# A fused attention and MLP kernel: weight sums of the last two groups taken straight from the joined weights, and the work of batch 0 placed anew

## Chip, cores and metric

The kernel runs on one core of a Trainium2 chip. The metric is device time in microseconds (us), the median of several executions. A core has five engines that work side by side and wait for each other through semaphores: TensorE (PE) for matmuls, VectorE (DVE) and ScalarE (ACT) for elementwise work, GpSimd (POOL) for elementwise work too, and SyncE (SP), which here only issues transfers. ACT issues some transfers as well. Each engine works through its own instructions in the order in which the program gives them.

## Reference

Clustered attention is followed by a mixing MLP. Queries and keys are each given to one of 16 clusters, and a query sees the keys of its own cluster only; the second part mixes tokens with a low rank matrix and then applies a two-layer MLP to each token. Shapes: 4 batches, 8 heads, 768 tokens, head dimension 64, model dimension 512, hidden dimension 2048.

```
scores = where(q_assign == k_assign, q @ k.T / 8, -1e9)
x = softmax(scores) @ v              # 4 x 768 x 512, heads side by side
u = x + ((x.T @ U) @ V).T            # U: 768 x 32, V: 32 x 768
out = u + relu(u @ w_ch1) @ w_ch2    # 512 x 2048 and 2048 x 512
```

U, V and both weight matrices are given as doubles.

## The kernel before

**Attention.** 16 units (batch times pair of heads), 12 steps each, make x batch by batch. Step numbers are the clock of the whole plan: M0 = 193 is the step at which batch 0's MLP begins, while the mixing of the last batch's tokens is still to come.

**The order.** A plan is written by hand: `at(time, function, arguments)` notes a call, all calls are sorted by their time and made in that order, and `keep_order` fixes that every engine keeps it. The times are numbers in tables (`mixes`, `stages`) and in the loops behind them. When something really runs follows from the waits: a function that stands early in an engine's order and has to wait holds up all that stands behind it on that engine.

**Precision.** A product in full precision is made of three matmuls: each operand is split into a high half, rounded to the matmul's format, and a low half, the rest (high x high, high x low, low x high). A matmul instruction is 128 x 128 against 384 or 512 columns.

**Batch 0's MLP.** It runs in two halves of 384 tokens (i = 0 and 1), each of 16 steps f, one for each 128 hidden units. A step has `gemm1(i, f)` (12 matmuls of 384 columns, L598 to L600), a relu on ACT that writes the high half of the hidden units (L606), the low half on DVE (L607), and `gemm2(i, f)` (9 matmuls of 512 columns, L617 to L619) that adds to y. In the plan gemm1 of the next step stands ahead of gemm2 of this one.

**The weights.** They come in four groups of four hidden blocks, and each group has eight tiles of 128 x 512, four of w1 and four of w2. `load_weights(g, step, stage)` makes a tile in four stages: a transfer of the doubles as 64-bit words (`rw`, L151, on ACT's queue for groups 2 and 3), a multiplication of the upper words on ACT (`rw_g`, L159), the `join` of both words on DVE (L169, L170, L172), whose result stands in PSUM (`ps_t`) for groups 2 and 3, and at last the high half as a cast on ACT and the low half as a subtraction on DVE (L190, L191). Groups 2 and 3, 16 tiles, are made in the first half of batch 0, one tile a step.

**The weight sums.** Batches 1 to 3 use a form with seven products in place of eight (Strassen's, in Winograd's variant), which needs sums and differences of quarters of the weights. A "turn" n makes them for one group g and one matrix k (0 for w1, 1 for w2). `recover` (L656 to L660) puts the weight together again from its halves, one quarter at a time: a copy of the low half to PSUM on ACT (L659), and an addition on DVE (L660) that writes a piece of the buffer `f`. `combine` (L662 to L671) makes four sums on POOL, `split_high` (L676) and `split_low` (L680) split them on ACT and POOL, and `store_sum` (L684, L685) writes both halves to the scratch `wc` in DRAM. Two of the places for high halves are the buffers `rw_t`. `store_block` (L643) writes the quarters that need no sum. The eight turns ran in the order of the groups, 3.1 steps apart from M0 + 3, the last one at M0 + 26.3.

**The tokens of batch 1.** `fetch_half` (L738) reads half of the mixed tokens into `st`, `turn_half` (L743) turns them on PE and copies them on ACT (L744), `u_sums` (L756) makes differences of quarters on DVE, in buffers of a ring to which `rw_t` belongs too, and `u_halves` (L761 to L767) splits quarters and differences on ACT and POOL. `fetch_w1` (L771) and `fetch_w2` (L783) read weight sums back. The low halves of batch 1's hidden units are made on POOL (L862).

**The last mix.** `mix_u`, `mix_sum` and `mix_v` for batch 3 run in the first half too: L533 to L550, with six additions on DVE into xt (L550) and a store to `u_scr`.

Of the kernel before, what the change touches and what calls it, by code (L numbers as in the profile page):

```python
# [40 lines left out]
B, H, S, D, C = 4, 8, 768, 64, 16  # L41
# [7 lines left out]
HT = NT // 2  # L49
ND = DM // P  # L50
NF = DF // P
NG = 4
# [35 lines left out]

mixes = {
    "mix_u":    ( 18.88,  18.35,  18.48,  16.57),  # L90
    "mix_sum":  ( 19.11,   19.1,  19.15,  18.35),
    "mix_v":    (  20.5,   20.4,  20.68,  19.42),
}


# [1 line left out]
    "mix":  (  3.36,   6.22,  15.04,  16.96),  # L97
    "g0":   ( 35.66,  38.22,  42.54,  52.94),
    "g1":   (-26.11, -21.73,  -20.5, -18.29),
    "g2":   ( -1.25,      0,    0.4,    0.7),  # L100
    "g3":   (  6.75,      8,    8.4,    8.7),
}

spots = [0.66, -0.06, 1.8, 2.25, 1.26, 2.09, 2.97, 3, 3.49, 3.81, 4.58, 5.03]
# [13 lines left out]
def clustered_attention_moe(ctx: ExitStack, tc: tile.TileContext, qk, v, cen, moe_U, moe_V, w1, w2, out):  # L118
# [3 lines left out]
    nc = tc.nc  # L122
# [21 lines left out]
    u_scr = [dram.tile([P, NT, DM], F32, name=f"u_scr{b}") for b in range(B)]  # L144

    def fetch(srcs, n, queue=nc.sync):

        step = srcs[0].shape[0]
        rw = raw.tile([P, 512], I64, name="rw")[0:step * len(srcs), 0:n]
        for i, src in enumerate(srcs):  # L150
            queue.dma_start(out=rw[i * step:(i + 1) * step], in_=src)  # L151
        return rw

    def upper(rw):

        r, n = rw.shape
        g = raw.tile([P, 512], F32, name="rw_g")[0:r, 0:n]
        high = rw.bitcast(I32).rearrange("p (n two) -> p n two", two=2)[:, :, 1].bitcast(F32)
        nc.scalar.mul(g, high, 2.0 ** -112)  # L159
        return rw, g.bitcast(I32)  # L160
# [15 lines left out]
    parts, pool = {}, {}  # L176

    def load_weights(g, step, stage):

        k, i = divmod(step, 4)  # L180
        if stage == 0:
            parts[g, step] = fetch([(w1, w2)[k][g, :, i, :]], 512, nc.scalar if g > 1 else nc.sync)
        elif stage == 1:
            parts[g, step] = upper(parts[g, step])
        elif stage == 2:
            parts[g, step] = join(*parts[g, step], g > 1)
        else:
            w = parts.pop((g, step))[2].bitcast(F32)
            hi, lo = wg[g][2 * k][:, i, :], wg[g][2 * k + 1][:, i, :]
            nc.scalar.copy(hi, w)  # L190
            (nc.vector if g > 1 or g == 1 and step in (1, 2, 3, 5) else nc.gpsimd).tensor_sub(lo, w, hi)  # L191


    def weight_tile(g, name, pool):
# [116 lines left out]
    n = B * NP  # L311
# [318 lines left out]
    B11, B12, B21, B22, T1, T2, T3, T4 = "B11", "B12", "B21", "B22", "T1", "T2", "T3", "T4"  # L630
# [10 lines left out]
    def store_block(k, g, name, part):  # L641

        nc.sync.dma_start(out=wc[k][g][:, :, slot[k][name], part * 256:part * 256 + 256],  # L643
                          in_=blocks(k, g, part)[name].bitcast(F32))

    def temps(n):
        at = 3072 * (n % 2 == 0 or n > 5)
        return [pool["f"][:, at + 512 * j:at + 512 * j + 512].rearrange("p (a n) -> p a n", a=2) for j in range(4)]

    def high_of(n, j):  # L650
        f = pool["f"]
        places = [f[:, 5120:5632], f[:, 5632:6144], *pool["o"], f[:, 2048:2560], f[:, 2560:3072]]
        count["o"] += 1
        return places[count["o"] % (6 if n < 6 else 4)].rearrange("p (a n) -> p a n", a=2)

    def recover(n, k, g, j):  # L656
        hi, lo = (blocks(k, g, part)[("A21", "A11", "A22", "A12")[j]] for part in range(2))
# [33 lines left out]
    spare, count = [], {"bank": 0, "f": 0, "o": 0}  # L691
# [43 lines left out]
        return ps[:, 0:HS]  # L735

    def fetch_half(b, h):
        nc.sync.dma_start(out=pool["st"], in_=u_scr[b][:, h * HT:(h + 1) * HT, :])  # L738

    def turn_half(b, h, d):  # L740
        ps = work("ps_uT")[:, 0:HS] if b == 1 else bank()
# [4 lines left out]
    def u_block(b, key):  # L746
        k, t = int(key[1]) - 1, int(key[2]) - 1
        return pool["ys"][1 - b % 2][:, 2 * k:2 * k + 2, t]
# [9 lines left out]
    def u_halves(b, key):  # L758
        if key[0] == "B":
            hi, lo = uc[key][:, 0], uc[key][:, 1]  # L760
            nc.scalar.copy(hi, u_block(b, key))  # L761
            nc.gpsimd.tensor_sub(lo, u_block(b, key), hi)
        else:
            for k in range(2):
                x = live["t", key, k]
                nc.scalar.copy(uc[key][:, 0, k], x)
                nc.gpsimd.tensor_sub(uc[key][:, 1, k], x, uc[key][:, 0, k])  # L767
# [168 lines left out]
    M0 = NS * n + 1  # L936
    plan = []

    def at(time, fn, *args):
        plan.append((time, len(plan), fn, args))  # L940
# [27 lines left out]
    for i in range(n):  # L968
# [10 lines left out]
        pace = (0.5, 0.75, 0.75, 1)[min(i, 3)]  # L979
        for u in range(NT if i == 0 else 0, NS):  # L980
            for h in range(2):
                if i < 3:
                    at(when("rowmax", i) + pace * u + 0.01 * h, rowmax, i, u, h)
                else:
                    g, r = divmod(2 * u + h, 2 * GV)
# [7 lines left out]
        for k in range(NS):  # L993
            h, c = divmod(k, NT)
# [10 lines left out]
    for b, (t_u, t_sum, t_v) in enumerate(zip(*mixes.values())):  # L1005
        o = NS * (NP * b + NP - 1)
        at(o + t_u, mix_u, b)
        at(o + t_sum, mix_sum, b)
        for t in range(NT):
            at(o + t_v + (t if b < B - 1 else t // HT), mix_v, b, t)  # L1010


    for k in range(3):
# [2 lines left out]
    for g, pace in enumerate((NS, 2.04, 1, 1)):  # L1016
        for stage, step in enumerate(stages[f"g{g}"]):
            for k in range(8):
                at(step + pace * k + (M0 if g else 0), load_weights, g, k, stage)

    at(M0 - 0.75, open_mlp)
    at(M0 + 8.05, open_weights)
# [8 lines left out]
            at(m + f + (1.2 if i == 0 or f < NF - 1 else 1.45), gemm2, i, f)  # L1031
        at(m + (16.35 if i == 0 else 16.47), finish, i)

    for n_, (g, k) in enumerate((g, k) for g in range(NG) for k in range(2)):
        c = M0 + (3 + 3.1 * n_ if n_ < 7 else 26.3)
        for r in range(4):
            at(c + 0.4 * r, recover, n_, k, g, r)
            at(c + (0.9, 1.4, 1.75, 2.1)[r], combine, n_, r)
            at(c + (1.9, 2.25, 2.6, 2.8)[r], split_high, n_, r)
            at(c + (2.4, 2.7, 3.0, 3.3)[r], split_low, n_, r)  # L1040
            at(c + (2.8, 3.1, 3.4, 3.7)[r], store_sum, n_, k, g, r)
        for r, name in enumerate(("A11", "A12", "A22")):
            for half in range(2):
                x = 2 * r + half
                since = (95, 142, M0 - 9, M0 - 2.5)
                at(since[n_] + (6 if g == 0 else 0.9) * x if g < 2 else M0 + 15.5 + 3.3 * (n_ - 4) + 0.55 * x,
                   store_block, k, g, name, half)

    at(M0 + 18, open_sevens)
    at(M0 + 31.3, free_rows)  # L1050
# [2 lines left out]
    for b in range(1, B):  # L1053
        o = M0 + NF * nh + 28 * (b - 1)
        if b == 1:
            fetched, turns = (o - 13.9, o - 6.4), (o - 7.7, o - 5.4)
        else:
            fetched, turns = (o - 20, o - 14), (o - 15.7, o - 8.7)
        for h in range(2):
            at(fetched[h], fetch_half, b, h)  # L1060
            for d in range(ND):
                at(turns[h] + 0.4 * d, turn_half, b, h, d)
        for k, key in enumerate((T1, T2, T3, T4)):
            for r in range(2):
                at((o - 4.9 if b > 1 else o - 3.9) + (k + 0.5 * r) * (1 if b > 1 else 0.8), u_sums, b, key, r)
        for key, when_ in ((B11, -4.95), (T1, -4.2), (B21, -3.7), (T2, -3.2), (B22, -2.7), (T3, -2.2), (T4, -1.2)):
            at(o + when_ * (1 if b > 1 else 0.8), u_halves, b, key)

        seq = [(1, 0), (1, 1), (1, 2), (2, 0), (1, 3), (2, 1), (1, 4), (2, 2), (1, 5), (2, 3),
               (1, 6), (2, 4), (1, 7), (2, 5), (2, 6), (2, 7)]  # L1070
        for k, (which, x) in enumerate(seq):
            t = o + 7 * U * k
            for s in range(7):
                if which == 1:
                    at(t + U * s, seven1, b, x, s)
                    at(t + U * s + 0.28, after1, b, x, s)
                else:
                    m, e = x // 2, 7 * (x % 2) + s
                    at(t + U * s, seven2, b, m, e)
                    at(t + U * s + 0.27, after2, b, m, e)  # L1080
            if which == 1:
                for key, sums, high, low in ((B22, None, 1.2, 1.25), (B11, None, 1.45, 1.5), (B21, None, 1.7, 2.6),
                                             (T3, 1.81, 2.0, 2.1), (T1, 1.95, 2.15, 2.4), (T2, 2.09, 2.3, 2.35),
                                             (T4, 2.23, 2.56, 2.6)):
                    if sums:
                        at(t + sums, h_sums, b, x, key)
                    at(t + high, h_high, b, x, key)
                    at(t + low, h_low, b, x, key)
                if x + 2 < 8 or b < B - 1:
                    for s0, s1 in ((0, 4), (4, 7)):  # L1090
                        at(t + U * s1 + 0.02, fetch_w1, (x + 2) % 8, s0, s1)
            elif x < 6 or b < B - 1:
                first = sorted(order[1].index(key) for key in order[b < B - 1][0:3])
                slots = [k for k in range(7) if (k in first) == (x % 2 == 0)]
                for K in range(2):
                    at(t + 7 * U + 0.01 * K, fetch_w2, (x - x % 2 + 2 + K) % 8, *slots)
        if b < B - 1:
            for j, when_ in enumerate((0.02, 0.1, 5, 5.3, 5.1, 5.45, 5.6, 5.9)):
                at(o + 28 + when_, join_up, b, j)
# [38 lines left out]
```

## Time and profile before

| | us |
|---|---|
| three executions | 1010.62, 1011.31, 1015.38 |
| their median | 1011.31 |
| the profiled execution | 1008.9 |
| its span in the profile | 1007.1 |
| batch 0's first half, first gemm1 to last gemm2 | 466.54 to 558.42 |
| batch 0's second half, up to batch 1's first product | 560.53 to 634.84 |

All rows are of the profiled execution, and their times count from the start of its span. A row of a timeline has its start, its duration, the engine, the line, and what it writes and reads; in brackets stands how long the engine was idle before it, and what ended that. A window gives the busy time of each engine in a stretch, and the TensorE clock that was granted as a share of full speed. In the list of waits, "y L617 <- ACT hx L606" reads: the matmul at L617 that writes y waited for ACT's row at L606 that writes hx. Matmuls overlap, so that their durations (0.34 and 0.40 us) are longer than their distances (0.174 and 0.232 us).

### The profile page before, as it was taken

How to read it: one execution, taken by the hardware profiler on the slowest of the kernel's cores; microseconds unless marked ns; L12 is line 12 of the kernel's file. 1: busy time of each engine (PE TensorE's matmuls, PEld its weight loads, DVE VectorE, ACT ScalarE, POOL GpSimd, SP SyncE). 2: the span in 40 equal slices, each digit the busy share in tenths (PEclk: the TensorE clock that was granted, in tenths of full speed). 3: DMA queues.
4: the chain of work that ended last, by engine and by line, in shares of the span. 5: the costliest groups of instructions: out<-in, count | busy, mean ns of one | idle time of the engine just before them, and what ended most of it. 6: DMA issues, size and time to landing. Idle time of an engine off the chain costs nothing. (4 is left out here: it accounts for less than half of the span.)

```text
span 1007.1 us, 15377 instructions
## 1 busy us (share of the span) xinstructions
PE 953.1 (95%) x5368; PEld 778.0 (77%) x5368; DVE 715.1 (71%) x1322; ACT 472.0 (47%) x837; POOL 601.5 (60%) x453
## 2 busy tenths in 40 slices
PE   5899999999999999988988998999999899999997
PEld 3565665676666756656777887899999899999997
DVE  5797777777787667666788524765688666886767
ACT  4454555565555645464456534453344433443330
POOL 5466676889678868753356846742375623855330
PEclk9899999999999999989999999999999999999999
DMA  7754653655676644347477995877677776677744
GB/s 183 193 130 119 162 148 93 201 156 151 152 213 170 153 116 144 96 134 235 142 232 232 322 349 187 329 266 271 231 261 260 274 295 239 229 280 267 248 147 146
DMA packets 76733, 205.29 MB, mean 204 GB/s; under 512 B 8624, under 2 KB 42416, under 8 KB 71792
## 3 DMA queue, kind: packets, MB, share of 16 engines
q1 hardware_dynamic: 73968, 195.82, 60.9%
q10 hardware_dynamic: 2688, 8.49, 2.8%
q8 instruction: 42, 0.69, 0.3%
q14 instruction: 35, 0.29, 0.1%
HBM read 131.07 MB, written 41.94 MB: 172 GB/s over the span
## 5 line engine op out<-in xcount | busy, mean ns | idle before, releaser
L442 DVE TENSOR_REDUCE m<-ps_max 128x1 f32<-128x384 f32 x384 | 195.5, 549 | 82.6 <-PE ps_max L440 81.2
L479 POOL TENSOR_TENSOR T<-T,pr 128x768 f32<-128x768 f32 x120 | 225.7, 1881 | 46.1 <-ACT pr L469 19.5
L469 ACT ACTIVATE pr<-st 128x768 f32<-128x768 f32 x192 | 154.6, 813 | 85.7 <-PE st L466 69.0
L487 PE MATMUL o_ps<-pr,vt 128*64 128x384 f32 x768 | 132.9, 496 | 0.1
L440 PE MATMUL ps_max<-arena 128*128 128x384 f32 x384 | 126.6, 380 | 6.7 <-DVE oh L356 2.5
L464 PE MATMUL st<-arena 128*128 128x384 f32 x384 | 105.0, 354 | 1.9 <-ACT pr L469 1.8
L440 PEld LDWEIGHTS ps_max<-arena 128*128 128x128 f32 x384 | 70.5, 192 | 45.4 <-issue 21.4
L487 PEld LDWEIGHTS o_ps<-pr,vt 128*64 128x64 f32 x768 | 52.9, 138 | 66.9 <-issue 60.3
L466 PE MATMUL st<-arena 97*128 97x384 f32 x384 | 99.7, 341 | 4.6 <-DMA arena<-mT 2.6
L479 POOL TENSOR_TENSOR T<-pr 128x768 f32<-128x768 f32 x30 | 56.6, 1885 | 64.9 <-ACT pr L469 64.9
L464 PEld LDWEIGHTS st<-arena 128*128 128x128 f32 x384 | 66.3, 190 | 17.8 <-issue 9.9
L466 PEld LDWEIGHTS st<-arena 97*128 97x128 f32 x384 | 70.4, 190 | 6.2 <-issue 4.5
L491 ACT COPY os<-o_ps 128x384 f32<-128x384 f32 x32 | 15.4, 480 | 105.4 <-PE o_ps L487 105.4
L800 PE MATMUL ps_p<-arena,w 128*128 128x384 f32 x186 | 62.3, 335 | 0.1
L801 PE MATMUL ps_p<-arena,w 128*128 128x384 f32 x186 | 62.2, 334 | 0.0
L802 PE MATMUL ps_p<-arena,w 128*128 128x384 f32 x186 | 62.2, 334 | 0.0
L800 PE MATMUL ps_q<-arena,w 128*128 128x384 f32 x150 | 50.1, 334 | 0.0
L802 PE MATMUL ps_q<-arena,w 128*128 128x384 f32 x150 | 50.1, 334 | 0.0
L801 PE MATMUL ps_q<-arena,w 128*128 128x384 f32 x150 | 50.1, 334 | 0.0
L380 POOL TENSOR_TENSOR arena<-R,arena 128x768 fp32r<-128x768 f32 x18 | 34.4, 1918 | 13.5 <-ACT arena L375 7.9
L665 POOL TENSOR_TENSOR f<-f 128x512 f32<-128x512 f32 x8 | 10.3, 1293 | 52.1 <-DVE f L660 52.1
L607 DVE SCALAR_TENSOR_TENSOR hx<-ps_h,hx 128x384 fp32r<-128x384 f32 x32 | 17.7, 554 | 29.0 <-ACT hx L606 28.9
(541 smaller groups left out, 2444.3 us busy)
## 6 DMA issues: line engine op xcount, KB each, us to landing
w<-wc SPq DMA_DIRECT2D x24, 1024.0 KB
w<-wc SPq DMA_DIRECT2D x24, 768.0 KB
wc<-f SPq DMA_DIRECT2D x52, 256.0 KB
arena<-wc SPq DMA_DIRECT2D x17, 768.0 KB
R<-in_qk SPq DMA_DIRECT2D x32, 384.0 KB
arena<-arena SPq DMA_DIRECT2D x32, 384.0 KB
arena<-arena SPq DMA_DIRECT2D x64, 192.0 KB
arena<-wc SPq DMA_DIRECT2D x10, 1024.0 KB
```

The lines of the kernel that those rows point to most:

```text
L380: eng.tensor_sub(part(X2[i % 3], 0, h), live["R", i][:, 2 * h:2 * h + 2].rearrange("p j q -> p (j q)"), part(X1[i % 3], 0, h))
L440: nc.tensor.matmul(ps[:, 0:HS], x1[:, 0, g // 2, g % 2, t * P:(t + 1) * P], x1[:, 1, h, g % 2, :], start=True, stop=True)
L442: nc.vector.reduce_max(live["m2", i][:, h, u:u + 1], ps[:, 0:HS], axis=AX.X)
L464: nc.tensor.matmul(st[:, j, 0:HS], x1[:, 1, hk, j, ks], x1[:, 0, h, j, :], start=True, stop=False)
L466: nc.tensor.matmul(st[:, j, 0:HS], x2[0:97, 1, hk, j, ks], x2[0:97, 0, h, j, :], start=False, stop=True)
L469: nc.scalar.activation(pr, st[:, :, 0:HS], AF.Exp, scale=SCALE)
L479: eng.tensor_add(T, live["p", i, h, 0] if c == 1 else T, live["p", i, h, c])
L487: nc.tensor.matmul(o_ps[64 * j:64 * j + 64, 0:HS], vv[:, c, j, :], pr[:, j, :], start=(c == 0), stop=(c == NT - 1))
L607: nc.vector.scalar_tensor_tensor(out=hl, in0=ps[:, 0:HS], scalar=0.0, in1=hh, op0=ALU.max, op1=ALU.subtract)
L800: nc.tensor.matmul(ps, w[:, 0, k], u[:, 0, k], start=(k == 0), stop=False)
L801: nc.tensor.matmul(ps, w[:, 0, k], u[:, 1, k], start=False, stop=False)
L802: nc.tensor.matmul(ps, w[:, 1, k], u[:, 0, k], start=False, stop=(k == 1))
```

## The change

**Sums from the joined weights.** `keep_joined` is new. For groups 2 and 3 it copies the joined weight on ACT straight from PSUM to the places in `f` from which `combine` starts. `recover` remains for groups 0 and 1 alone; 16 copies and 16 additions of it go, and 16 copies come. The turns of groups 2 and 3 come first (`turns_of`); as their tiles must be joined first, turn 0 stands at M0 + 2.5, and each next one four steps later. Groups 0 and 1 follow in the second half. `temps` and `high_of` are changed to fit the new places.

**The joins** of groups 2 and 3 start earlier in their steps (`stages`), and the first two loads three steps earlier still.

**The last mix** has its second part 0.7 steps earlier, and its six last products two by two, from 18.42 on, where they stood three by three from 19.42.

**The tokens of batch 1.** The fetch of half 1 is issued by ACT in place of SP, and the turning of both halves is placed anew. The subtraction for one quarter (B11) goes from POOL to DVE.

**The last turn.** Its `combine`, `split` and `store` parts wait 5.9 steps more, and so stand behind the start of batch 1's products. `store_block` has new times.

```diff
 mixes = {
-    "mix_sum":  ( 19.11,   19.1,  19.15,  18.35),
-    "mix_v":    (  20.5,   20.4,  20.68,  19.42),
+    "mix_sum":  ( 19.11,   19.1,  19.15,  17.65),
+    "mix_v":    (  20.5,   20.4,  20.68,  18.42),
...
-    "g2":   ( -1.25,      0,    0.4,    0.7),
-    "g3":   (  6.75,      8,    8.4,    8.7),
+    "g2":   ( -1.75,  -0.44,  -0.28,   0.25),
+    "g3":   (  6.25,   7.56,   7.72,   8.25),
...
             nc.scalar.copy(hi, w)
             (nc.vector if g > 1 or g == 1 and step in (1, 2, 3, 5) else nc.gpsimd).tensor_sub(lo, w, hi)
+            if g > 1:
+                keep_joined(turns_of.index((g, k)), i, w)
...
+    turns_of = [(2, 0), (2, 1), (3, 0), (3, 1), (0, 0), (0, 1), (1, 0), (1, 1)]
+
+    def keep_joined(n, i, w):
+
+        at = 3072 * (n % 2 == 0)
+        f = pool["f"][:, at:at + 2048].rearrange("p (c k a n) -> p c k a n", c=2, k=2, a=2)
+        to = f[:, i // 2, :, i % 2] if n % 2 else f[:, :, 1 - i // 2, i % 2]
+        nc.scalar.copy(to, w.rearrange("p (c n) -> p c n", c=2))
...
-        nc.sync.dma_start(out=pool["st"], in_=u_scr[b][:, h * HT:(h + 1) * HT, :])
+        (nc.scalar if b == 1 and h else nc.sync).dma_start(out=pool["st"], in_=u_scr[b][:, h * HT:(h + 1) * HT, :])
...
-            nc.gpsimd.tensor_sub(lo, u_block(b, key), hi)
+            (nc.vector if b == 1 and key == B11 else nc.gpsimd).tensor_sub(lo, u_block(b, key), hi)
...
-            at(o + t_v + (t if b < B - 1 else t // HT), mix_v, b, t)
+            at(o + t_v + (t if b < B - 1 else 0.45 * t), mix_v, b, t)
...
-                at(step + pace * k + (M0 if g else 0), load_weights, g, k, stage)
+                ahead = 3 if g == 2 and stage == 0 and k < 2 else 0
+                at(step + pace * k + (M0 if g else 0) - ahead, load_weights, g, k, stage)
...
-    for n_, (g, k) in enumerate((g, k) for g in range(NG) for k in range(2)):
-        c = M0 + (3 + 3.1 * n_ if n_ < 7 else 26.3)
+    for n_, (g, k) in enumerate(turns_of):
+        c = M0 + (2.5, 6.5, 10.5, 14.5, 17.3, 20.0, 22.7, 26.4)[n_]
+        if n_ > 3:
+            for r in range(4):
+                at(c + 0.3 * r, recover, n_, k, g, r)
+        wait = 5.9 if n_ == 7 else 0
         for r in range(4):
-            at(c + 0.4 * r, recover, n_, k, g, r)
-            at(c + (0.9, 1.4, 1.75, 2.1)[r], combine, n_, r)
...
+            at(c + wait + (0.9, 1.4, 1.75, 2.1)[r], combine, n_, r)
...
-            fetched, turns = (o - 13.9, o - 6.4), (o - 7.7, o - 5.4)
+            fetched, turns = (o - 13.9, o - 6.45), (o - 7.9, o - 5.1)
```

**What moves, in three places.** The rows that follow give line, operation, what is written and read, and the shape; a DMA row is the issue of a transfer. Line numbers are each kernel's own.

First place: ACT, in the first steps of the first half. `hx` are relus, `rw` loads of a later tile, `rw_g` the multiplied upper words, `arena<-ps_t` the high cast. Before:

```order
L159 ACTIVATE rw_g<-rw 128x512
L501 COPY sums<-ps_sum 128x384
L606 ACTIVATE hx_5005<-ps_h 128x384
L190 CAST arena<-ps_t 128x512
L151 DMA rw<-in_w 128x512
L159 ACTIVATE rw_g<-rw 128x512
L606 ACTIVATE hx_5006<-ps_h 128x384
```

and of the change, for the second tile, with the kept copy at L655:

```order
L608 ACTIVATE hx_5007<-ps_h 128x384
L159 ACTIVATE rw_g<-rw 128x512
L151 DMA rw<-in_w 128x512
L190 CAST arena<-ps_t 128x512
L655 COPY f<-ps_t 128x2x256
L608 ACTIVATE hx_5008<-ps_h 128x384
```

The issue of the load moves from behind the cast to ahead of it, and waits there for the third join, which still reads the buffer that it fills. Between the cast and the relu comes the kept copy, which waits for DVE's subtraction of the low half; the next rw_g moves from behind the cast to behind the relu.

Second place: the token fetch of half 1 in the second half, `st<-u_scr`. Before it stands on SP, among stores of sums (L684, L685) and blocks (L643) and fetches of w1 (L771):

```order
L684 DMA wc_3_97<-f 256x1x256
L685 DMA wc_3_97<-f 256x1x256
L643 DMA wc_3_101<-w2h_5409 256x1x256
L738 DMA st<-u_scr_90 128x1536
L643 DMA wc_3_101<-w2l_5410 256x1x256
L771 DMA w_93<-wc_0_94 128x2048
```

and of the change on ACT, between copies of turned tokens (L756), a split copy (L688), relus (L608) and a recovery (L671):

```order
L756 COPY f<-ps_uT 128x384
L608 ACTIVATE hx_5008<-ps_h 128x384
L688 CAST f<-f 128x512
L750 DMA st<-u_scr_90 128x1536
L671 COPY ps_r<-arena 128x512
L608 ACTIVATE hx_5009<-ps_h 128x384
```

It leaves SP's queue, with the stores ahead of it, and stands behind one relu and one split copy on ACT. On PE the first tokens of that half are turned behind the same gemm2 (f = 9) as before.

Third place: POOL, at the end of batch 0. Before, the last turn's combinations (L665 to L671) and low halves (L680) stand among the low halves of the tokens (L762, L767):

```order
L665 TENSOR_TENSOR f<-f 128x512
L667 TENSOR_TENSOR f<-f 128x512
L762 TENSOR_TENSOR arena<-f,arena 128x768
L669 TENSOR_TENSOR f<-f 128x512
L671 TENSOR_TENSOR f<-f 128x512
L767 TENSOR_TENSOR arena<-rw,arena 128x384 x2
L680 TENSOR_TENSOR f<-f 128x512
```

and of the change behind them, among the low halves of batch 1's hidden units (L874):

```order
L779 TENSOR_TENSOR arena<-rw,arena 128x384
L677 TENSOR_TENSOR f<-f 128x512
L874 TENSOR_TENSOR arena<-rw_g,arena 128x384
L874 TENSOR_TENSOR arena<-rw,arena 128x384
L679 TENSOR_TENSOR f<-f 128x512
L681 TENSOR_TENSOR f<-f 128x512
L874 TENSOR_TENSOR w2l_5005<-rw_g,w2l_5005 128x384
L874 TENSOR_TENSOR u_5006<-rw_t,u_5006 128x384
L683 TENSOR_TENSOR f<-f 128x512
```

The eight operations of the last turn move past those of the tokens into the stretch in which the products of batch 1 run.

More of the change, by code (lines that the diff above doesn't have):

```diff
@@ L644, in store_block @@
                           in_=blocks(k, g, part)[name].bitcast(F32))
+    turns_of = [(2, 0), (2, 1), (3, 0), (3, 1), (0, 0), (0, 1), (1, 0), (1, 1)]
[4 more added lines that the diff above has]
+        nc.scalar.copy(to, w.rearrange("p (c n) -> p c n", c=2))
     def temps(n):
         at = 3072 * (n % 2 == 0 or n > 5)
-        return [pool["f"][:, at + 512 * j:at + 512 * j + 512].rearrange("p (a n) -> p a n", a=2) for j in range(4)]
+        return [pool["f"][:, at + 512 * j:at + 512 * j + 512].rearrange("p (a n) -> p a n", a=2)
+                for j in ((1, 0, 3, 2) if n % 2 else range(4))]
     def high_of(n, j):
@@ L653, in high_of @@
         count["o"] += 1
-        return places[count["o"] % (6 if n < 6 else 4)].rearrange("p (a n) -> p a n", a=2)
+        return places[count["o"] % (6 if n < 6 else 4 if n < 7 else 2)].rearrange("p (a n) -> p a n", a=2)
     def recover(n, k, g, j):
@@ L1032, in clustered_attention_moe @@
         at(m + (16.35 if i == 0 else 16.47), finish, i)
-    for n_, (g, k) in enumerate((g, k) for g in range(NG) for k in range(2)):
-        c = M0 + (3 + 3.1 * n_ if n_ < 7 else 26.3)
-        for r in range(4):
-            at(c + 0.4 * r, recover, n_, k, g, r)
-            at(c + (0.9, 1.4, 1.75, 2.1)[r], combine, n_, r)
-            at(c + (1.9, 2.25, 2.6, 2.8)[r], split_high, n_, r)
-            at(c + (2.4, 2.7, 3.0, 3.3)[r], split_low, n_, r)
-            at(c + (2.8, 3.1, 3.4, 3.7)[r], store_sum, n_, k, g, r)
+    for n_, (g, k) in enumerate(turns_of):
[4 more added lines that the diff above has]
+        wait = 5.9 if n_ == 7 else 0
+        for r in range(4):
+            at(c + wait + (0.9, 1.4, 1.75, 2.1)[r], combine, n_, r)
+            at(c + wait + (1.9, 2.25, *((3.1, 3.4) if wait else (2.6, 2.8)))[r], split_high, n_, r)
+            at(c + wait + (2.4, 2.7, *((3.5, 3.8) if wait else (3.0, 3.3)))[r], split_low, n_, r)
+            at(c + wait + (2.8, 3.05, *((3.9, 4.2) if wait else (3.4, 3.7)))[r], store_sum, n_, k, g, r)
         for r, name in enumerate(("A11", "A12", "A22")):
@@ L1044, in clustered_attention_moe @@
                 x = 2 * r + half
-                since = (95, 142, M0 - 9, M0 - 2.5)
-                at(since[n_] + (6 if g == 0 else 0.9) * x if g < 2 else M0 + 15.5 + 3.3 * (n_ - 4) + 0.55 * x,
-                   store_block, k, g, name, half)
+                since = (95, 142, M0 - 9, M0 - 2.5, M0 + 9, M0 + 11.5, M0 + 14.5, M0 + 17.5)[2 * g + k]
+                at(since + (6 if g == 0 else 0.9 if g == 1 else 0.35) * x, store_block, k, g, name, half)
     at(M0 + 18, open_sevens)
```

## Prediction, made before the changed kernel ran

> **What bounds the kernel now.** I read the page's busy shares first, then the list of what TensorE (PE) waits for in batch 0, then windows by stage, then single rows. The page:
>
> ```profile
> span 1007.1 us, 15377 instructions
> PE 953.1 (95%) x5368; PEld 778.0 (77%) x5368; DVE 715.1 (71%) x1322; ACT 472.0 (47%) x837; POOL 601.5 (60%) x453
> ```
>
> PE is busy for 953 of 1007 us, and the change leaves its work as it is. Only time in which PE waits, or runs at a low clock, can be won. Its waits from 466 to 640 us, which is batch 0's MLP with the weights made beside it (engine, tile, line, what it waited for: total, times, longest):
>
> ```profile
> PE y L619 <- DVE hx L607: 4.9, 4, 1.6
> PE ps_h L549 <- DVE xt L550: 3.5, 2, 2.6
> PE y L617 <- ACT hx L606: 3.5, 2, 2.2
> PE ps_uT L743 <- DMA st<-u_scr: 3.1, 1, 3.1
> PE y L618 <- DVE w2l L191: 1.4, 2, 1.0
> ```
>
> These are 16.4 us. The windows show where (stretch, length, busy time of PE, PEld, DVE, ACT and POOL, granted clock, DMA share, GB/s):
>
> ```profile
> 466.50:558.40 91.90, 80.23 (x388) 65.63 (x389) 70.13 (x115) 47.26 (x91) 42.52 (x33) 0.98 0.63 205
> 520.00:540.00 20.00, 18.48 (x95) 16.30 (x95) 14.67 (x25) 12.69 (x24) 12.69 (x10) 1.00 0.87 285
> 560.00:603.00 43.00, 43.00 (x222) 38.96 (x222) 15.11 (x25) 18.43 (x37) 29.82 (x24) 1.00 1.03 343
> 606.90:611.00 4.10, 4.02 (x16) 4.02 (x17) 0.69 (x1) 0.97 (x2) 1.28 (x1) 0.58 1.00 387
> 631.00:635.00 4.00, 3.91 (x10) 3.06 (x11) 2.96 (x4) 1.45 (x4) 4.00 (x3) 0.57 0.45 150
> ```
>
> The first half lasts 91.9 us with PE busy for 80.2: 11.7 us idle. From 560 to 603 PE never stops. Then come two stalls, each followed by 4 us at a clock of 0.57 or 0.58:
>
> ```profile
> 600.24 0.59 SPq L738 DMA_DIRECT2D st<-u_scr  x1
> 606.98 0.56 PE L743 MATMUL ps_uT<-ident,st 128*128 128x128 f32 x3 [3.09 <-DMA st<-u_scr]
> 631.09 0.70 PE L617 MATMUL y<-w2h,hx 128*128 128x512 f32 x1 [2.23 <-ACT hx L606]
> ```
>
> **First half: what goes.** The recoveries of groups 0 and 1 move to the second half, where those of groups 2 and 3 vanish. DVE loses these here:
>
> ```profile
> L660 DVE TENSOR_TENSOR f<-ps_r,arena 128x512 f32<-128x512 f32 x9 | 6.2, 687 | 5.5 <-DMA u_scr<-xt 1.5 <-POOL f L680 1.3 <-POOL f L665 1.3
> L660 DVE TENSOR_TENSOR f<-ps_r,w 128x512 f32<-128x512 f32 x8 | 5.5, 688 | 2.7 <-ACT ps_r L659 2.6
> ```
>
> That is 6.2 + 5.5 = 11.7 of its 70.1 us. By shares alone one would expect PE's idle time to shrink.
>
> **First half: what comes.** The kept copy stands behind the subtraction of the low half and waits for it; the relu and the next tile's rw_g stand behind the copy on ACT. So a circle closes that was open before: rw_g (ACT), three joins (DVE), high cast (ACT), low subtraction (DVE), kept copy, relu, next rw_g (ACT). Its links, from the first tile of before:
>
> ```profile
> 471.76 0.66 ACT L159 ACTIVATE rw_g<-rw 128x512 f32<-128x512 f32 x1 [4.76 <-DMA rw<-in_w]
> 474.65 0.59 ACT L190 CAST arena<-ps_t 128x512 fp32r<-128x512 f32 x1 [1.46 <-DVE ps_t L172]
> 474.71 0.34 ACTq L151 DMA_DIRECT2D rw<-in_w  x1
> 475.13 0.67 ACT L159 ACTIVATE rw_g<-rw 128x512 f32<-128x512 f32 x1
> 475.26 0.69 DVE L191 TENSOR_TENSOR arena<-ps_t,arena 128x512 fp32r<-128x512 f32 x1 [0.19 <-ACT arena L190]
> ```
>
> Here the next rw_g followed the cast after 0.48 us, and the subtraction ran beside it. In the changed order: rw_g to cast 2.89 (471.76 to 474.65), cast to subtraction 0.61 (474.65 to 475.26), the subtraction 0.69 with 0.02 to hand over (as between the cast's end, 475.24, and 475.26), then on ACT the copy and the relu, whose distances these rows give:
>
> ```profile
> 487.74 0.59 ACT L659 COPY ps_r<-w 128x512 f32<-128x512 f32 x1 [0.83 <-DVE f L660]
> 488.26 0.48 ACT L606 ACTIVATE hx<-ps_h 128x384 fp32r<-128x384 f32 x1
> 562.90 0.49 ACT L606 ACTIVATE hx<-ps_h 128x384 fp32r<-128x384 f32 x1 [1.23 <-PE ps_h L600]
> 567.08 0.49 ACT L606 ACTIVATE hx<-ps_h 128x384 fp32r<-128x384 f32 x1 [1.64 <-PE ps_h L600]
> 567.47 0.59 ACT L659 COPY ps_r<-w2l 128x512 f32<-128x512 f32 x1
> ```
>
> Copy to relu 0.52, relu to the next operation 0.39. One turn: 2.89 + 0.61 + 0.71 + 0.52 + 0.39 = 5.12 us. PE's own step is shorter: where ACT waited for PE alone, two relus lie 4.18 us apart (562.90 and 567.08).
>
> ACT also issues the load of a later tile. In 12 of the 16 steps that issue now stands ahead of the cast and waits for the third join, whose input it overwrites. What it costs, a row of the attention part shows, where an issue on ACT had an operation ready behind it:
>
> ```profile
> 218.73 0.73 ACTq L217 DMA_DIRECT2D arena<-mT  x1
> 219.56 0.81 ACT L469 ACTIVATE pr<-st 128x768 f32<-128x768 f32 x1 [0.86 <-PE ps_max L440]
> ```
>
> That operation began 0.10 us after the issue ended. With the 0.34 us of a weight load it is 0.44, in 12 steps 5.3 us. The other end is nothing, if the cast gets past the issue; I take 5.3, since ACT works in order.
>
> Other work stands between the links, by my estimate from such distances 7.0 us: six split copies between kept copy and relu (0.52 each, 3.1), the copy of sums (0.36), x3 and its subtraction (1.0), the part of three mix additions that DVE has ahead of a subtraction (0.96) and four casts of turned tokens (0.4 each, 1.6). Sum: 16 x 5.12 + 5.3 + 7.0 = 94.2 us. The circle starts when ACT has cast the last tokens, at 467.0; the half ended with the last gemm2:
>
> ```profile
> 466.49 0.51 ACT L589 CAST arena<-ps_uT 128x384 fp32r<-128x384 f32 x1
> 558.42 0.40 PE L617 MATMUL y<-w2h,hx 128*128 128x512 f32 x1
> ```
>
> 467.0 + 94.2 = 561.2, and that gemm2 starts about 0.1 later: 561.3 in place of 558.42. **First half: +2.9 us.** The loads asked for three steps earlier take away ACT's 4.76 us wait above, which this start assumes. The idle time is now spread over the steps, under 1.7 us each, and I count no slow clock: the wait of 1.5 us in the window from 520 to 540 left the clock at 1.00.
>
> [...]
>
> **Second half.** ACT issues the token fetch of half 1 behind a relu and one split copy, some 1.0 us after that relu starts (0.39 + 0.52 and the hand-over); SP had it behind stores. The relu starts 0.3 us after its gemm1, and PE then has half a step three times, 6.3 us, before it turns the tokens: 5.0 us of cover. Landing took 6.7 us (600.24 to 606.98) with the DMA engines full. A wait of 0 to 1.7 us is left; I take 0.7, since the transfers around it are partly moved ahead. Won: 3.1 - 0.7 = 2.4, and the slow clock after the old wait, 4.1 x 0.42 = 1.7.
>
> The 2.23 us stall at 631 has another origin:
>
> ```profile
> 628.34 1.70 DVE L756 TENSOR_TENSOR rw_t<-f 128x384 f32<-128x384 f32 x1 [2.91 <-DMA wc<-rw_t]
> 630.13 0.51 ACT L766 CAST arena<-rw_t 128x384 fp32r<-128x384 f32 x1 [4.15 <-DVE rw_t L756]
> 630.55 0.48 ACT L606 ACTIVATE hx<-ps_h 128x384 fp32r<-128x384 f32 x1
> ```
>
> A difference of tokens needs the buffer rw_t, which holds a sum of the last turn until its store has landed; ACT waits for the difference, and the relu stands behind. Now the last turn's splits come after the tokens, and the turn before starts 3.7 steps (15 us) earlier. The stall goes: 2.2, and 4.0 x 0.43 = 1.7 of clock. **Second half: -8.0 us** (-4 if only one of the two goes, -9 if the fetch is in time).
>
> [...]
>
> **Start of batch 1.** The last turn's eight POOL operations now lie among the low halves of the products:
>
> ```profile
> L665 POOL TENSOR_TENSOR f<-f 128x512 f32<-128x512 f32 x8 | 10.3, 1293 | 52.1 <-DVE f L660 52.1
> 640.00:662.00 22.00, 21.85 (x126) 21.53 (x125) 18.60 (x37) 11.85 (x26) 12.72 (x13) 1.00 0.95 359
> ```
>
> 8 x 1.29 = 10.3 us; POOL is idle for 9.3 of these 22 us, and one subtraction of its own (B11) goes to DVE. On SP the last turn's stores stand between fetches of w1. I take 0; the bounds are 0 and +10.3, if all of it stands in front of what PE needs.
>
> **Sum**: 1008.9 + 2.9 - 8.0 + 0 = 1003.8 us for the profiled execution (1007.1 of span and 1.8 around it). The median of the runs shown, 1011.3, is 2.4 above it, so the forecast is 1006.2.
>
> **Rivals.** (A) The circle is shorter than I sum. Without the 5.3 of the issues the time is 1000.9; with PE as the bound, all 11.7 us of idle time won where I count 2.9 lost, 991.6. For it: DVE loses work, and PE needs 80.2 us. Against: the order ties each link to the one before. (B) The circle is longer and outweighs the second half. Its place is ACT's queue between cast and relu: split copies wait there for POOL's combinations of 1.29 us, load issues for the landing of stores. Each 0.3 us per turn costs 4.8; from 0.3 on the gain is gone, and 0.75 gives 1018.2. For it: I see only 2 to 3 us of slack at the twelfth issue; against: most combinations are a whole turn ahead. (C) Little comes of it: one of the second half's stalls stays (the fetch lands late from ACT too), or POOL takes 4 to 5 us back in batch 1: 1010 to 1011.
>
> **Chances.** Forecast 0.43 (1002 to 1010 by itself), A 0.27 (991 to 1002), B 0.16 (1012 to 1020), C 0.14. The range 994 to 1016 leaves out the low end of A and the high end of B. Half a per cent, 5.1 us, is about what a measurement of this kernel can tell from no change: below 1006.2 lie A and half of the forecast, 0.48; above 1016.4 most of B, 0.13; between them 0.39.
>
> **What would show it.** First half: rw_g rows 5.1 to 5.6 us apart, kept copies with idle time before them that DVE ends, PE waiting for hx at nearly every step, the last gemm2 starting near 561.3; before 556 speaks for A, after 566 for B. Second half: no PE wait over 1 us on st, none on hx near 631, a clock of 1.00 in both places. Batch 1: no PE wait on POOL in its first 40 us. The prediction is wrong if the first half gets shorter, or if one of the two stalls stays.

## The result, and the profile after

The changed kernel takes 1018.4 us (median of 9 runs, 1015.6 to 1020.7), the kernel before beside it 1011.6 (9 runs, 1009.8 to 1015.4): ratio 1.0058, interval 1.0039 to 1.0077. It became slower, by 0.6 per cent, and the interval does not contain 1; the forecast was 1006.2 us. The profiled execution took 1018.0 us.

The page of the changed kernel, its first lines:

```profile
span 1016.2 us, 15354 instructions
PE 953.8 (94%) x5368; PEld 778.8 (77%) x5368; DVE 707.8 (70%) x1307; ACT 472.4 (46%) x837; POOL 598.9 (59%) x452
```

DVE has 7 us less to do, PE as much as before, and the span is 9 us longer. The windows of the changed kernel: first half, second half, batch 1 up to the first turned tokens of batch 2's second half, and a short stretch (same columns as before):

```profile
468.30:567.00 98.70, 80.86 (x388) 67.17 (x389) 61.22 (x97) 43.72 (x84) 33.89 (x27) 0.97 0.64 210
567.00:641.50 74.50, 69.74 (x351) 61.95 (x350) 30.26 (x45) 34.12 (x66) 52.02 (x41) 0.98 0.76 265
641.50:728.80 87.30, 85.55 (x490) 83.96 (x489) 56.09 (x109) 37.34 (x82) 41.74 (x41) 1.00 0.75 271
624.00:628.50 4.50, 3.86 (x13) 2.87 (x13) 3.64 (x7) 3.36 (x8) 0.34 (x1) 0.72 0.98 411
```

Three stages can be set against the kernel before by the same rows (first gemm1, last gemm2 of the first half, first product of batch 1, first turned tokens of batch 2's second half):

| stage | before | after | difference | forecast |
|---|---|---|---|---|
| first half | 91.9 | 98.7 | +6.8 | +2.9 |
| second half | 76.4 | 74.5 | -1.9 | -8.0 |
| batch 1 | 85.8 | 87.4 | +1.6 | 0 |

That is +6.4 us (from unrounded times), close to the difference of the medians, 6.8. The rest of the 9 us, 1.8 ahead of the first half and 0.9 behind batch 1, is scatter between executions: in the runs 1 to 9 and 11 below, whose attention part is the same, the first half begins anywhere from 465.8 to 468.6.

**First half.** PE's waits in it, of the changed kernel:

```profile
PE ps_h L600 <- ACT f L655: 9.3, 6, 2.3
PE y L619 <- ACT hx L608: 3.8, 2, 3.0
PE ps_h L551 <- ACT f L655: 3.0, 2, 2.3
PE ps_oT L522 <- ACT f L655: 1.1, 1, 1.1
```

13.4 us of PE's waits end with a kept copy (L655). It isn't the relu, as I had written: gemm1 needs a PSUM buffer, and the kept copy is the last reader of the one whose turn it is. That leaves two readings. Either the copy holds a buffer that PE lacks, or the whole round on ACT and DVE is too long and PE meets it at this place. The rows of ACT (start, duration, engine, line, what it does):

```profile
479.87 0.67 ACT L159 ACTIVATE rw_g<-rw 128x512 f32<-128x512 f32 x1
482.82 0.33 ACTq L151 DMA_DIRECT2D rw<-in_w  x1
483.20 0.59 ACT L190 CAST arena<-ps_t 128x512 fp32r<-128x512 f32 x1 [2.65 <-DVE xt L523]
484.54 0.59 ACT L655 COPY f<-ps_t 128x512 f32<-128x512 f32 x1 [0.76 <-DVE arena L191]
485.02 0.50 ACT L608 ACTIVATE hx<-ps_h 128x384 fp32r<-128x384 f32 x1
485.41 0.68 ACT L159 ACTIVATE rw_g<-rw 128x512 f32<-128x512 f32 x1
504.25 0.67 ACT L159 ACTIVATE rw_g<-rw 128x512 f32<-128x512 f32 x1
509.35 0.67 ACT L159 ACTIVATE rw_g<-rw 128x512 f32<-128x512 f32 x1
```

From 479.87 to 485.41 a turn of the circle takes 5.54 us; from 504.25 to 509.35, where the load is issued behind the cast, 5.10. ACT never waits for PE here: the kept copy waits 0.76 us for the subtraction, and the cast for DVE.

**Second half.** The stall near 631 is gone, the wait for the tokens is 1.8 in place of 3.1 us, and a wait of 3.0 is new. Behind it stand, on ACT, DVE and PE of the changed kernel:

```profile
605.91 0.48 ACT L756 COPY f<-ps_uT 128x384 f32<-128x384 f32 x1 [3.96 <-DMA wc<-f]
622.86 0.69 DVE L672 TENSOR_TENSOR f<-ps_r,arena 128x512 f32<-128x512 f32 x1 [6.59 <-DMA wc<-f]
623.59 0.59 ACT L671 COPY ps_r<-arena 128x512 f32<-128x512 f32 x1 [6.69 <-DVE f L672]
624.64 0.55 PE L755 MATMUL ps_uT<-ident,st 128*128 128x128 f32 x3 [2.98 <-ACT f L756]
```

Read from below: PE needs a buffer that a token copy on ACT (L756) must read first; that copy stands behind a recovery's copy (L671), which waits for an addition on DVE, which has waited 6.6 us until a store out of the same piece of `f` had landed. That store was issued at 614.95, and late for a reason that the first row shows: the copy at 605.91 had waited 4.0 us for another landing, and the split copies behind it, which the later stores need, began only at 606.29. The kernel before has no such waits: its recoveries' additions lose 0.7 us to landing stores in the second half, those of the changed kernel 11.2. The window from 624.0 to 628.5 above shows the clock at 0.72 after PE's wait.

### The profile page after: what moved, and what is told of

Same layout as the page of the kernel before. It is cut to its first block, busy times and chain, and to the rows that moved or that the text cites. A ratio compares the mean times of both kernels' runs of the same rounds, so it can differ in the third digit from the quotient of the medians.

```text
span 1016.2 us, 15354 instructions
## 1 busy us (share of the span) xinstructions
PE 953.8 (94%) x5368; PEld 778.8 (77%) x5368; DVE 707.8 (70%) x1307; ACT 472.4 (46%) x837; POOL 598.9 (59%) x452
## 5 line engine op out<-in xcount | busy, mean ns | idle before, releaser
L609 DVE SCALAR_TENSOR_TENSOR hx<-ps_h,hx 128x384 fp32r<-128x384 f32 x32 | 17.8, 556 | 41.0 <-ACT hx L608 40.9
L692 POOL TENSOR_TENSOR f<-f 128x512 fp32r<-128x512 f32 x22 | 28.2, 1295 | 14.1 <-ACT f L688 14.1
```

## The experiments

The ninth and the tenth run were timed in rounds against the kernel before; all others are single executions. Stages are in us, first half, second half, batch 1; the changed kernel has 98.7, 74.5 and 87.4. Where an edit leaves a half alone, that half shows the scatter: the first takes 98.7 to 99.9 us (runs 4 to 6), the second 72.9 to 75.1 (runs 1 to 3), batch 1 87.3 to 87.4.

**1. The kept copy behind the next rw_g.** It tells the two readings of PE's waits apart: the circle gets shorter, and the buffer is held for longer.

```diff
-            if g > 1:
-                keep_joined(turns_of.index((g, k)), i, w)
+            if g > 1:
+                live["w", g, step] = turns_of.index((g, k)), i, w
...
+                if g > 1 and stage == 3:
+                    at(step + pace * k + M0 + 0.35, keep_late, g, k)
...
-        c = M0 + (2.5, 6.5, 10.5, 14.5, 17.3, 20.0, 22.7, 26.4)[n_]
+        c = M0 + (2.8, 6.8, 10.8, 14.8, 17.3, 20.0, 22.7, 26.4)[n_]
```

> The kept copy moves from ahead of the relu to behind the next tile's rw_g on ACT (the sums of the first four turns 0.3 steps later, so that they stay behind it). Theory circle (the round of rw_g, joins, cast, subtraction, kept copy, relu sets the first half): the copy and the subtraction leave the round, a turn falls from 5.5 to 4.2 to 4.6 us, and the first half, first gemm1 to last gemm2, from 98.7 to 80 to 86 us. Theory bank (PE waits because the kept copy holds a PSUM bank that a gemm1 needs): the bank is held for longer, PE's waits on the kept copy grow from 13 us in all, and the first half stays at 98 us or gets longer.

Measured: 90.8, 74.9, 87.4; 1007.2 us. The waits on the kept copy are gone from PE's list in the first half, whose first rows are now:

```profile
PE ps_h L600 <- DVE hx L609: 6.3, 3, 3.4
PE ps_h L551 <- DVE xt L552: 2.3, 2, 1.5
PE ps_h L600 <- ACT sums L503: 1.3, 1, 1.3
```

The half falls by 7.9 us although the buffer is held longer (5.6 us in the mean from the first join to its last reader, 4.7 in the changed kernel), so the time for which it is held isn't what bound the half. The fall is less than expected (80 to 86): PE now waits for the last reader of a relu's buffer on DVE (L609), which stands behind DVE's joins. The half is still some 12 us above PE's own 78.9; run 7 shows that 3.1 of them are the load issue, and what sets the rest was not tested.

**2. The load issue behind the kept copy.**

```diff
-    "g2":   ( -1.75,  -0.44,  -0.28,   0.25),
-    "g3":   (  6.25,   7.56,   7.72,   8.25),
+    "g2":   ( -1.73,  -0.44,  -0.28,   0.25),
+    "g3":   (  6.27,   7.56,   7.72,   8.25),
```

> The issue of the weight loads on ACT moves from ahead of the high cast to behind the kept copy, nothing else. Theory circle: 0.38 to 0.44 us less in each of 12 turns, the first half 94 us in place of 98.7 (93 to 95). Rival (the issue is hidden beside the joins): no change, 98 to 99.5.

Measured: 95.0, 75.1, 87.4; 1017.1 us. The first half loses 3.7 us, 0.31 for each of 12 issues, a little less than expected. So the issue did stand in the circle.

**3. The kept copy ahead of the subtraction.**

```diff
             nc.scalar.copy(hi, w)
+            if g > 1:
+                keep_joined(turns_of.index((g, k)), i, w)
             (nc.vector if g > 1 or g == 1 and step in (1, 2, 3, 5) else nc.gpsimd).tensor_sub(lo, w, hi)
-            if g > 1:
-                keep_joined(turns_of.index((g, k)), i, w)
```

> The kept copy stands ahead of the subtraction of the low half, which now waits for it, in place of the other way round. Theory circle: the relu no longer waits for DVE, but DVE comes to the next joins later; a turn of some 5.0 us, the first half 89 to 92 us. Rival (the order of these two does not matter, since both still follow each other): 98 to 99.

Measured: 91.4, 72.9, 87.4; 1010.4 us. The first half loses 7.3 us, as the circle gives. Two readers of one tile, put the other way round: the relu no longer waits for DVE. The second half has the wait of 3.0 us on the token copy still, at 616.53, but the clock after it stays at 1.00 here (the last section shows how the wait fell).

**4. The last turn's recovery later.** It reads the weights of group 1 when the halves of the tokens have begun to take their place, so the last turn's sums have other values in this kernel.

```diff
-                at(c + 0.3 * r, recover, n_, k, g, r)
+                at(c + (2.6 if n_ == 7 else 0) + 0.3 * r, recover, n_, k, g, r)
```

> The recovery of the last turn stands 2.6 steps later; the first half is left as it is. Theory landing (in the second half DVE stands at the last turn's additions until stores of the turn before have landed, and copies of tokens and a relu stand behind them on ACT): the 3.0 us wait of PE on the token copy near 624 us and the slow clock after it go, and the second half, last gemm2 of the first half to the first product of batch 1, falls from 74.5 to 69 to 71.5 us. Rival (the wait comes from the late token fetch and its crowded transfers): the wait stays within 1 us, the second half at 73 to 75.

Measured: 99.9, 69.0, 87.4; 1012.5 us. The wait of 3.0 us is gone, and the second half has lost 5.5 us, its clock at 1.00: it was DVE's wait for the landing. The wait on the tokens, now PE's only one in that half, stayed:

```profile
PE ps_uT L755 <- DMA st<-u_scr: 1.3, 1, 1.3
```

**5. The fetches of w1 later.** Why did stores of 256 KB land so late? They are queued on SP behind the first fetches of w1 (two transfers of 1.8 MB together, at 593.05) and behind each other, six stores of 256 KB up to 597.79.

```diff
-            at(M0 + 23 + 3 * K, fetch_w1, K, s0, s1)
+            at(M0 + 27 + 1.5 * K, fetch_w1, K, s0, s1)
```

> The first fetches of w1 for batch 1 (3.7 MB in two blocks) stand 4 and 2.5 steps later on SP, behind the stores of the turns of the second half. Theory crowding (those fetches fill the DMA engines for some 9 us each, so that stores of sums queued behind them land late, and a token copy on ACT and the last turn's additions on DVE wait for these landings): the 4.0 us wait of ACT near 602 us and the 6.6 us wait of DVE near 616 shrink below 2 us, PE's wait of 3.0 us on the token copy goes, and the second half falls from 74.5 to 69 to 71.5 us with all results computed. Rival (landing takes as long without the fetches): 73.5 to 75.

Measured: 99.4, 69.5, 87.3; 1012.3 us. PE's only wait in the second half is now the one on the tokens, and the clock stays at 1.00:

```profile
PE ps_uT L755 <- DMA st<-u_scr: 1.8, 1, 1.8
```

The window of its second half:

```profile
565.60:635.10 69.50, 67.74 (x350) 60.88 (x349) 30.55 (x45) 33.69 (x66) 50.76 (x41) 1.00 0.80 284
```

In the changed kernel the first pair of fetches kept the DMA engines busy for some 6 us, not the 9 of the expectation: from 594 to 600 us they moved 1.94 MB, with 252 of the 405 packets of 6 KB or more, and from 600 to 606 us 1.58 MB, with 1617 of the 1622 packets under 2 KB.

The expected gain is there, 5.0 us, and here nothing is left out. Not all of the chain went as expected: ACT's wait of 4.0 us for a landing is gone, but DVE still waits 4.2 us at one addition, for a store that was issued 5.5 us before it (7.9 in the changed kernel). It waits earlier in the half, where nothing that PE needs stands behind it.

**6. The last turn not put off.** In this kernel the high halves of its last two sums overwrite those of the first two before these are stored, so some of the last turn's sums have other values.

```diff
-        wait = 5.9 if n_ == 7 else 0
+        wait = 0
```

> The last turn's sums no longer wait 5.9 steps; they stand at the end of batch 0, as before the change. Theory late turn (its split copies on ACT and its operations on POOL among batch 1's products cost PE 1.5 us there): batch 1, first product to the first turned tokens of batch 2, falls from 87.4 to 85.8 us, while the stall of the kernel before near the end of the second half comes back, the second half 76 to 79 us. Rival (the 1.5 us come from the B11 subtraction on DVE or from the transfers): batch 1 stays at 87.2 to 87.5.

Measured: 98.8, 81.9, 85.4; 1024.2 us. Batch 1 is back at the time of before (85.8), so the last turn's operations cost 2.0 us there, and the subtraction on DVE, which stayed, costs nothing that shows. The second half costs more than expected, with PE waiting for a relu again:

```profile
PE y L619 <- ACT hx L608: 4.5, 1, 4.5
PE ps_uT L755 <- ACT f L756: 3.4, 1, 3.4
```

It isn't the stall of the kernel before, which came from a token difference that waited for a store. Here a split copy of the last turn waits for low halves on POOL, and the relu at 639.15 stands behind it:

```profile
637.80 0.62 ACT L688 CAST f<-f 128x512 fp32r<-128x512 f32 x1 [3.13 <-POOL f L692]
```

The last turn has two places for its high halves in the changed kernel, where it had four before, so this wait belongs in part to the edit itself. The half is 7.4 us longer than in the changed kernel; how much putting the last turn off is worth against the kernel before, this run does not tell.

**7 and 8. Together.** The seventh has the edits of 1 and 5 and the load issue behind the cast (as in 2), the eighth those of 3, 2 and 5.

> Kept copy behind the next rw_g, load issue behind the cast, fetches of w1 later. Theory circle with theory crowding, adding up: first half 86 to 89 us (90.8 with the late copy alone, less up to 4 for the issue), second half 69 to 72, in all about 1000 to 1003 us. Rival (the late copy has taken PE to another bound, a bank that DVE's low half of the relu frees): first half 90 to 91.5.

> Kept copy ahead of the subtraction, load issue behind both, fetches of w1 later. Theory circle: first half 87 to 89 us (91.4 less 3.7 for the issue), second half 69 to 72, in all 1000 to 1004 us. Rival (with the copy first the issue lies beside the subtraction already and costs nothing): first half 90.5 to 91.5.

Measured: 87.7, 69.3, 87.4 and 1000.7 us for the seventh; 87.9, 69.5, 87.4 and 1003.3 us for the eighth. The parts add up: 3.1 us for the issue in the seventh, 3.5 in the eighth.

**9. The seventh again, against the kernel before, in five rounds.**

> The kernel with the late copy, the load issue behind the cast and the later fetches of w1 again, now in rounds against the kernel before. Theories circle and crowding: the gain of the single look holds, ratio 0.985 to 0.992, first half 87 to 88.5 us, second half 69 to 70. Rival (the single look was a good execution): ratio 0.993 to 1.000.

Measured: 1001.0 us (4 runs, 1000.4 to 1001.5) against 1012.1 (13 runs), ratio 0.9898, interval 0.9882 to 0.9915. It beats the kernel before by 1.0 per cent, and so the changed kernel too, which is slower than that. Its windows, first and second half:

```profile
468.00:555.30 87.30, 78.49 (x388) 66.21 (x389) 60.25 (x97) 42.48 (x84) 33.69 (x27) 0.98 0.70 236
555.30:624.50 69.20, 67.69 (x350) 60.85 (x349) 30.46 (x44) 33.87 (x67) 50.81 (x41) 1.00 0.80 285
```

In the second half PE is busy for 67.7 of 69.2 us. In the first 8.8 us are left.

**10. The kernel before with the later fetches alone** (the edit of 5, three rounds), to see how much of this needs the change at all.

> The kernel before with nothing but the first fetches of w1 4 and 2.5 steps later. Theory crowding: its late token fetch lands in 3.5 to 5 us in place of 6.7, PE's wait on st falls from 3.1 to 0.3 to 2 us, the second half from 76.4 to 73 to 75.5, ratio 0.996 to 0.999; so most of the gain of the best version is not this edit. Rival (most of the gain is this edit alone): ratio below 0.994.

Measured: 1009.2 us (10 runs) against 1012.1, ratio 0.9968, interval 0.9953 to 0.9982. The wait on the tokens fell to 1.1 us, as expected. The second half ended after 70.3 us, earlier than expected, but batch 1 then took 90.9, as a wait moved there:

```profile
PE ps_uT L743 <- DMA st<-u_scr: 1.1, 1, 1.1
PE ps_p L800 <- DMA w<-wc: 3.1, 1, 3.1
```

So this edit brings 2.9 of the best version's 11.1 us by itself.

**11. The best version with the token fetch on SP.**

```diff
-        (nc.scalar if b == 1 and h else nc.sync).dma_start(out=pool["st"], in_=u_scr[b][:, h * HT:(h + 1) * HT, :])
+        nc.sync.dma_start(out=pool["st"], in_=u_scr[b][:, h * HT:(h + 1) * HT, :])
```

> The best version with the token fetch of half 1 issued by SP again, where it stands behind stores of sums. Theory queue (ACT issues it earlier than SP can, since SP waits there for POOL's low halves): PE's wait on st rises from 1.6 to 3 to 6 us, the second half from 69.3 to 71.5 to 76. Rival (the landing decides, not the issue): 69 to 70.5.

Measured: 86.9, 68.7, 87.4; 998.4 us. The expectation fell: SP issued the fetch at 595.19, 41.3 us after the last gemm2 of the first half, ACT (in run 9) at 596.81, 41.5 us after it, and PE waited 0.9 us in place of 1.5:

```profile
595.19 0.33 SPq L753 DMA_DIRECT2D st<-u_scr  x1
```

PE's wait for it:

```profile
PE ps_uT L758 <- DMA st<-u_scr: 0.9, 1, 0.9
```

With the fetches of w1 out of the way the move to ACT is worth nothing. What it is worth with the fetches where the changed kernel has them was not tested.

## Why the prediction was wrong

**The circle: right, and as long as worked out.** A turn was put at 5.12 us, 5.56 with the issue; the rows show 5.10 and 5.54. That the kept copy waits for the subtraction, and that this outweighs DVE's shorter work, held: runs 1 and 3 take 7.9 and 7.3 us away by moving that copy. The wait shows in the rows: the kept copy at 484.54 waits 0.76 us for the subtraction, and in run 3, where the order was turned round, the subtraction waits for the copy, in most turns 1.1 to 1.6 us. One sign was misread: PE's waits were to name the relu at nearly every step, and they name the kept copy.

**First half, +2.9 against +6.8: a term too small.** The term is the "other work between the links", 7.0 us by estimate. The circle ran from 468.16 to 566.35, 98.2 us; 12 x 5.54 and 4 x 5.10 are 86.9 of it, which leaves 11.3. Three rows of the changed kernel show most of the 4.3 us:

```profile
513.65 0.64 PE L551 MATMUL ps_h<-x,v 96*128 96x512 f32 x2
514.08 0.69 DVE L552 TENSOR_TENSOR xt<-ps_h,xt 128x512 f32<-128x512 f32 x1 [1.29 <-PE ps_h L551]
534.31 0.59 ACT L190 CAST w1h<-ps_t 128x512 fp32r<-128x512 f32 x1 [4.65 <-DMA wc<-arena]
```

A mix addition ahead of a subtraction did not only cost its own time: DVE stood there 1.29 us for a product of PE, which ran at 513.65, right behind a gemm2, and so the kept copy behind the subtraction came 1.8 us late (2.58 us of waiting in place of 0.76). With 0.6 us more in the next turn, where another addition stands ahead of the joins, the mix additions cost 2.4 us where 0.96 had been counted. And ahead of the cast at 534.31 a load issue waited for a store to land: the cast came 4.65 us after ACT's last work, where an undisturbed turn has 2.65, 2.0 us more; the next issue waited 0.4. No term of the sum had this. Rival B had named the wait, and the prediction had seen 2 to 3 us of slack; there was none.

**Second half, -8.0 against -1.9: the step that failed.** Both stalls were treated as wins to be subtracted, and I wrote of no new wait. The stall near 631 did go, and so did the wait that was behind it: the differences into `rw_t` begin without waiting for a store (no idle time in brackets):

```profile
633.09 1.37 DVE L768 TENSOR_TENSOR rw_t<-f 128x384 f32<-128x384 f32 x1
```

The wait on the tokens fell to 1.8 us, just past the end of the range given for it (0 to 1.7), where 0.7 had been taken. But the turn before the last and the last write the same pieces of `f`, and the recovery of the last had to wait, 6.6 us at one addition, for stores that stand on SP behind the fetches of w1, two pairs of 1.8 MB. The prediction followed what the moved code would free, and not what it would wait for itself. Runs 4 and 5 show it from both sides: with the recovery later, or the fetches later, the second half takes 69.0 and 69.5 us, 7.4 and 6.9 less than before. So the -8.0 were nearly there to be had; a new wait took some 5 of them, 3.0 as the wait itself and most of the rest as the slow clock after it. Neither of the two signs that the prediction gave for being wrong covers this: the first half did not get shorter, and one stall went while the other shrank.

**Batch 1, 0 against +1.6: inside the bounds, with the wrong value taken.** Run 6 gives 2.0 us for the last turn there. POOL had idle time enough (it was busy for 41.7 of 87.3 us), but the operations on ACT and POOL stand in order among those that PE needs. In the changed kernel PE waits there for ACT (0.5) and DVE (0.8), each less than a microsecond; together they are most of the 1.6. The first of them shows how: two split copies of the last turn (L688) wait on ACT for stores to land, and the copy behind them is what PE waits for at 665.08.

```profile
663.61 0.62 ACT L688 CAST f<-f 128x512 fp32r<-128x512 f32 x1 [1.27 <-DMA wc<-f]
```

**Slow clock.** I counted it by the windows of before, with 0.58 and 0.57 behind waits of 3.09 and 2.23 us. The new wait of 2.98 us was followed by a clock of 0.72 over 4.5 us, so here too a wait cost clock; but it is not the length of a wait alone that decides, as the last section shows. The first half, for which no slow clock was counted, has a clock of 0.97 (0.98 before); what that adds to its length was not separated.

**Rivals.** The time is that of rival B, and its place, waits for landing stores in ACT's queue, was part of it (2.4 us). The larger part is a wait for landing stores on DVE in the second half, which no rival had; that the time fell where B had put it is in part chance.

## What to carry to other kernels

When work leaves a busy engine, walk once round the loop that the remaining operations form across engines, each waiting for the last, and compare one turn with the bound engine's step: here 5.5 us against 4.2 mattered more than 11.7 us of DVE work saved. A copy that only has to happen some time belongs behind the operation that others wait for, not ahead of it. Before a stall is booked as won, list what the moved code itself will wait for, the landing of stores out of buffers that it reuses above all, and what is queued ahead of these stores.

## What the runs showed that I had not expected

The waits of PE name the last reader of a PSUM buffer, not the operation that makes the round long: in the changed kernel they name the kept copy (13.4 us), in run 1 the low half of the relu (6.3), and only the edits told which of them mattered.

Small stores landed late behind large fetches: the copy at 605.91 waited for a store that was issued at 597.79, 8 us earlier, behind two fetches and five other stores. With the fetches moved the half lost 5 us.

```profile
593.05 0.93 SPq L783 DMA_DIRECT2D w<-wc  x2
597.79 0.64 SPq L697 DMA_DIRECT2D wc<-f  x1
```

A wait of 2.27 us at 473.73 in the changed kernel left the clock at 1.00, one of 2.23 us at 631.09 before the change did not.

```profile
473.73 0.44 PE L600 MATMUL ps_h<-arena,w 128*128 128x384 f32 x1 [2.27 <-ACT f L655]
```

The traces show more. In all 13 of them the granted clock changes only at the borders of pieces of 3.41 us, which follow each other through the whole trace; in the kernel before, from 436.66 us on, the stretches of one clock last 6.83, 64.85, 3.41, 95.57, 3.41, 20.48, 3.41 and 368.64 us, each a whole number of pieces. The windows below are such pieces, two of the kernel before and three of the changed one:

```profile
627.81:631.22 3.41, 1.18 (x8) 0.86 (x7) 1.85 (x2) 0.90 (x2) 3.41 (x4) 1.00 0.56 190
631.22:634.63 3.41, 3.41 (x9) 2.60 (x10) 2.61 (x3) 1.28 (x3) 3.41 (x3) 0.50 0.35 118
```

```profile
468.95:472.36 3.41, 2.51 (x18) 1.56 (x16) 2.27 (x5) 0.59 (x1) 0.35 (x1) 1.00 0.46 168
472.36:475.77 3.41, 2.04 (x12) 2.04 (x13) 1.90 (x3) 1.92 (x4) 0.00 (x0) 1.00 0.49 149
475.77:479.19 3.42, 2.74 (x14) 2.06 (x13) 2.26 (x5) 0.77 (x2) 0.00 (x0) 1.00 0.29 44
```

The 2.23 us lie in one piece, in which PE is busy for 1.18 of 3.41 us, and the next piece runs at half the clock. The 2.27 us are cut by a border into 0.90 and 1.37, and no piece is slow. From 450 to 735 us of the 13 traces, each of the 23 pieces at full clock with more than 1.85 us of idle PE is followed by a slow one, and none with less than 1.76; in between both occur. Outside that stretch these two numbers don't hold: a piece with 1.64 us of idle PE (433.25, before) was followed by a slow one, one with 1.89 us (793.22, changed kernel) was not. So from 450 to 735 us it depended on where a wait of 2 to 3 us fell whether it cost another 1.7 us (half of 3.41): in run 3 the wait of 3.02 us was cut into 1.72 and 1.30 and cost nothing more, and its second half took 72.9 us in place of 74.5.
